# The state rows of an attention kernel with two MoE layers: the last four batch rows multiplied by the weights together in 64-row products, w_in's sums spread unevenly, three sets of PSUM banks

## The chip, the cores and the metric

The kernel runs on one core of a Trainium2 chip. TensorE (PE) multiplies, VectorE (DVE), ScalarE (ACT) and GpSimd (POOL) do the elementwise work, and all DMAs are issued by SyncE (SP). The metric is device time in microseconds (us) for one execution; lower is better. Every product of two float32 operands is made of three products of "fp32r" parts: each operand is split into a rounded high part and the low rest, and high·high, high·low and low·high are added in PSUM. TensorE's time is therefore mostly a count of 512-column matmuls, three for each product.

## What is computed

The reference, cut: cross attention between 512 tokens and 32 state rows per batch row and head, then a gated layer, then a second layer with a softmax gate and a normalisation.

```
x: 8 x 8 x 512 x 64 (batch B, head H, token, D)   state: 8 x 8 x 32 x 64
scores = x @ state.T / 8;    a  = softmax(scores);   xread = a @ state
scores2 = state @ x.T / 8;   a2 = softmax(scores2);  sread = a2 @ x
x = concat([xread, sread], axis=2) -> (8*544, 512)
x = (sigmoid(x @ w_gate) * (x @ w_val)) @ w_out            # 512 -> 1536 -> 512
h = x @ w_in                                               # 512 -> 1024
solu = h * softmax(h);  out = layernorm(solu) * g_ln @ w_out2    # 1024 -> 512
```

## The kernel before

**Stages.** A start-up stage loads and unpacks the weights and treats batch row 0. Then come blocks: rows 1 to 6, a block called SREAD (the 256 `sread` rows of all batch rows), and row 7, which I call the last block. A block runs over 12 chunks `c` of 128 hidden columns. After the last block comes the second layer, over 34 tiles of 128 tokens: four tiles of row 7 first, whose order the scheduler sets, then pairs of tiles in an order written by hand. In the blocks too the order on each engine is that of the program (`tc.manual_schedule`), so one late instruction holds up everything behind it on its engine.

**A chunk.** `first_mm` makes the gate's 128 x 512 product in PSUM bank `gps` and the value's in `vps`, 6 matmuls each. Its stationary operands `mh` and `ml` are not the weights but "states by weights": since xread = a @ state, the kernel multiplies the state rows of a batch row by w_gate and w_val beforehand (`state_w`, one of 12 products `n` = (p, g) of 128 x 512 for each batch row). `sigma` (ACT) reads `gps`, `gated` (DVE) reads `vps`; `gated_hi` (ACT) and `gated_lo` (DVE) split the result into `gh` and `gl`, and one chunk later `out_acc` adds it to the four banks `acc[0..3]` with 12 matmuls (`m` = 0 to 3). A step of the next row's attention (`parts[c]`) stands in each of the first ten chunks; step 4 holds the exponentials, which fill ACT. Its loads (`load_xq` into `e2t`, `load_row`) are issued by SP.

**States by weights.** `make` calls `state_w` at most once a chunk and stays at most three products ahead of their use. Rows 2 to 7 go in pairs: in the even row's turn the state blocks of two batch rows and of two heads fill the 128 x 128 stationary tile `sth`/`stl`, and two `mm3` (6 matmuls of 512 columns) give the product for both rows. Half of the contraction meets zeros there (`a_state_pair_split` fills only the blocks that belong together). What belongs to the odd row goes to DRAM (`msp`) by two 64-partition DMAs, and comes back by one 128-partition DMA (`state_load`) when that row needs it.

**The last block** also unpacks w_out2 (`conv.step`: four DVE instructions, some on ACT, and one POOL addition for each chunk, L223) and prepares sums of blocks of w_in (`w_pair_ops`: 24 steps, each with one DVE instruction, L644, L647 or L652), two for each chunk.

**The second layer.** `h2_out(i, f)` names the two banks of tile `i`. The first four tiles alternate between acc[0..1] and acc[2..3]; `chain(i)` (ACT and DVE) reads them. The pairs after them alternate between `[acc[0], acc[1], acc[2]]` and `[acc[3], gps, vps]`.

Of the kernel before, what the change touches and what calls it, by code (L numbers as in the profile page):

```python
# [19 lines left out]
EXPS = 7  # L20

# [5 lines left out]
def attn_moe_moe2_kernel(ctx: ExitStack, tc: tile.TileContext, x, state, w_gate, w_val, w_out, w_in2, w_out2, g_ln, out):  # L27
# [89 lines left out]
    ssp = tc.dram_tile([B, P, KC * NS], F32, name="ssp")  # L117
    msp = [tc.dram_tile([NF1, P, 512], F32, name=f"msp{b}") for b in range(B)]
# [172 lines left out]
    def paired(a):  # L291
        return 2 <= a < B and a - a % 2 + 1 < B
# [214 lines left out]
    def state_w(b, p, g, i, o, hi, o2=vps):  # L507
# [4 lines left out]
        if not paired(b):  # L512
# [3 lines left out]
        elif b % 2 == 0:  # L516
# [14 lines left out]
    def state_load(b, n):  # L531
        nc.sync.dma_start(out=spill[n % 4], in_=msp[b][n])
# [39 lines left out]
    def out_acc(c, n):  # L572
        h, l = woh[c], wol[c]
        i = c % 2
        for m in range(KC):
            sl = slice(m * P, (m + 1) * P)
            mm3(ps_acc(m, n), h[:, sl], l[:, sl], gh[i][:, 0:n], gl[i][:, 0:n], c == 0, c == NF1 - 1)
# [95 lines left out]
    def banks(i):  # L673
        return ([acc[0], acc[1], acc[2]], [acc[3], gps, vps])[i // 2 % 2]

    def h2_out(i, f):
        if tiles[i][0] == 0:
            return acc[2 * (i % 2) + f]
        a, b, c = banks(i)
        return ((b, c), (a, acc[3] if i + 1 == len(tiles) else b))[i % 2][f]  # L680
# [68 lines left out]
    def turn(i):  # L749
# [3 lines left out]
        if i >= nt - 2:  # L753
            for q, o in ((0, gps), (1, vps)):
# [71 lines left out]

    def loads(n):

        nonlocal loaded
        loaded = max(loaded, made - NF1)  # L830
        while loaded < min(made - NF1 + n, len(ring)):
            b, p, g = ring[loaded]
            if not paired(b) or b % 2 == 0:
                return
            state_load(b, 2 * p + g)
            loaded += 1
# [173 lines left out]
    with tc.manual_schedule():  # L1010
        for n_b, b in enumerate(blocks[1:], 1):
# [5 lines left out]
            if last:  # L1017
# [8 lines left out]
                x_late.close()  # L1026
                sbt = ctx.enter_context(tc.tile_pool(name="sbt", bufs=1, side="right"))
# [8 lines left out]
            nxt = blocks[n_b + 1] if not last else None  # L1036
            for c in range(NF1):
# [41 lines left out]
                if last:  # L1079
                    for _ in range(min(2, len(w_steps) - 1)):  # L1080
# [47 lines left out]
    with tc.manual_schedule():  # L1128
        for i in range(len(first), nt, 2):
# [33 lines left out]
            if end:  # L1163
                product(i, 7, o, False, False)
                plus(acc[3], o, tmp)
# [35 lines left out]
        for f in range(2):  # L1201
            d = slice(f * DO // 2, (f + 1) * DO // 2)
            out2(nt - 1, d=d, bank=(acc[0], att[(nt - 1) % 2])[f])
            store(nt - 1, d, (acc[0], att[(nt - 1) % 2])[f])
# [29 lines left out]
```

## Time and profile before

| what | value |
|---|---|
| median of 3 runs | 1124.13 us (1120.77 to 1129.18) |
| the profiled execution: its time, its span | 1122.8 us, 1121.0 us |
| PE busy | 1081.3 us (96%) |
| DVE, ACT, POOL busy | 773.3 (69%), 601.1 (54%), 384.0 (34%) us |
| mean granted TensorE clock | 0.996 of full speed |
| PE's share of the chain that ended last | 78% |

The profiled execution's time is 1.8 us above its span; the span runs from the first to the last instruction. Matmuls are pipelined: one of 512 columns is listed with some 390 ns, while the next one starts 227 ns later, so steps from start to start count, not durations.

### The profile page before, as it was taken

The numbers are of one execution on the slowest core, as the hardware profiler recorded it, in microseconds if no ns is written. First come the engines' busy times: TensorE is split into PE (matmuls) and PEld (weight loads), VectorE is DVE, ScalarE is ACT, GpSimd is POOL, SyncE is SP. The second block draws the span as 40 slices with busy tenths as digits, with TensorE's granted clock in tenths as the row PEclk, the third lists the DMA queues.
The fourth block names the chain that finished last, engine by engine and source line by source line (L and its number), as shares of the span: only waits on it lengthen the run. The fifth ranks groups of instructions, "written<-read, shape, count | busy, mean of one in ns | idle before, by whom it ended". The sixth has DMA issues, their size and how long they took to land.

```text
span 1121.0 us, 15909 instructions
## 1 busy us (share of the span) xinstructions
PE 1081.3 (96%) x5501; PEld 860.1 (77%) x5501; DVE 773.3 (69%) x1348; ACT 601.1 (54%) x1169; POOL 384.0 (34%) x445
## 2 busy tenths in 40 slices
PE   7787899999999999999999999989999999999998
PEld 5555567777878878878778898867888888888887
DVE  5999956367465476465575466997577777788773
ACT  5766545555445455543554454655565565565553
POOL 2777733300000000000000042226566666767551
PEclk9999999999999999999999999999999999999999
DMA  8764040231360331440521525411454453543441
GB/s 231 244 200 126 1 116 1 71 94 38 78 162 23 81 94 38 121 123 13 133 47 39 158 100 150 113 57 46 143 170 131 158 171 123 176 155 123 158 141 38
DMA packets 139600, 122.88 MB, mean 110 GB/s; under 512 B 71040, under 2 KB 111232, under 8 KB 139520
## 3 DMA queue, kind: packets, MB, share of 16 engines
q1 hardware_dynamic: 139520, 121.87, 37.0%
q8 instruction: 43, 0.70, 0.3%
q14 instruction: 37, 0.30, 0.1%
HBM read 78.32 MB, written 43.52 MB: 109 GB/s over the span
## 4 chain that ended last, share of the span: by engine, by line
PE 78%; DVE 13%; issue 3%; ACT 2%; DMA 1%; POOL 1%; SPq 0%; DVEq 0%; POOLq 0%; ACTq 0%
PE acc L138 11%; PE acc L140 10%; PE acc L139 10%; PE att L138 6%; PE att L140 6%; PE att L139 6%; PE gps L138 4%; PE gps L139 4%; PE gps L140 4%; PE vps L138 4%; PE vps L140 4%; PE vps L139 4%; DVE wf L213 2%; DVE wf L203 1%; DVE wf L206 1%
## 5 line engine op out<-in xcount | busy, mean ns | idle before, releaser
L138 PE MATMUL acc<-gh,woh 128*128 128x512 f32 (+1 forms) x432 | 168.6, 390 | 0.2 <-ACT gh L129 0.2
L139 PE MATMUL acc<-gl,woh 128*128 128x512 f32 (+1 forms) x432 | 164.7, 381 | 2.0 <-POOL gl L570 1.3
L564 DVE TENSOR_TENSOR sg<-vps,sg 128x512 f32<-128x512 f32 (+1 forms) x108 | 71.0, 658 | 135.4 <-PE vps L140 121.5
L140 PE MATMUL acc<-gh,wol 128*128 128x512 f32 (+1 forms) x432 | 164.3, 380 | 0.0
L560 ACT ACTIVATE sg<-gps 128x512 f32<-128x512 f32 (+1 forms) x108 | 61.6, 570 | 151.7 <-PE gps L140 147.2
L138 PEld LDWEIGHTS acc<-gh,woh 128*128 128x128 f32 x432 | 81.7, 189 | 31.4 <-issue 15.4
L223 POOL TENSOR_TENSOR tt<-tt,xn 128x512 int32<-128x512 int32 x16 | 23.5, 1466 | 215.5 <-PE vps L140 153.3
L139 PEld LDWEIGHTS acc<-gl,woh 128*128 128x128 f32 x432 | 81.8, 189 | 18.3 <-POOL gl L570 2.3
L256 POOL MEMSET xtr<- 32x256 f32 x18 | 5.4, 302 | 262.1 <-PE att L324 261.5
L140 PEld LDWEIGHTS acc<-gh,wol 128*128 128x128 f32 x432 | 81.7, 189 | 16.0
L129 ACT ACTIVATE gh<-sg 128x512 fp32r<-128x512 f32 (+1 forms) x101 | 60.4, 598 | 61.8 <-DVE sg L564 61.8
L775 POOL TENSOR_TENSOR wol<-ut,woh 128x512 fp32r<-128x512 f32 x48 | 61.6, 1299 | 86.9 <-ACT woh L129 86.9
L135 DVE TENSOR_TENSOR ml<-gps,mh 64x512 fp32r<-64x512 f32 (+2 forms) x57 | 38.7, 678 | 63.1 <-ACT stg L129 50.9
L138 PE MATMUL gps<-ah,mh 128*128 128x512 f32 x192 | 75.8, 395 | 5.1 <-DVE ml L135 3.9
L129 ACT ACTIVATE mh<-gps 64x512 fp32r<-64x512 f32 (+2 forms) x53 | 31.2, 589 | 90.7 <-PE gps L140 60.5
L138 PE MATMUL att<-woh,woh 128*128 128x512 f32 (+1 forms) x204 | 79.8, 391 | 0.0
L140 PE MATMUL att<-woh,wol 128*128 128x512 f32 (+1 forms) x204 | 79.4, 389 | 0.0
L139 PE MATMUL att<-wol,woh 128*128 128x512 f32 (+1 forms) x204 | 79.3, 389 | 0.0
L140 PE MATMUL gps<-ah,ml 128*128 128x512 f32 x192 | 75.4, 393 | 3.4 <-DVE ml L135 3.2
L138 PE MATMUL vps<-ah,mh 128*128 128x512 f32 x192 | 75.6, 394 | 1.1 <-DVE ml L135 1.1
L139 PE MATMUL gps<-al,mh 128*128 128x512 f32 x192 | 75.2, 392 | 0.9 <-DVE al L135 0.9
L570 DVE TENSOR_TENSOR gl<-sg,gh 128x512 fp32r<-128x512 f32 (+1 forms) x97 | 68.1, 702 | 10.9 <-ACT gh L129 6.9
(431 smaller groups left out, 2875.5 us busy)
## 6 DMA issues: line engine op xcount, KB each, us to landing
usp<-ub SPq DMA_DIRECT2D x32, 512.0 KB, 2.6
ut<-usp SPq DMA_DIRECT2D x128, 128.0 KB, 2.9
msp<-stg SPq DMA_DIRECT2D x72, 128.0 KB, 2.3
stg<-msp SPq DMA_DIRECT2D x36, 256.0 KB, 3.0
out_dram<-sg SPq DMA_DIRECT2D x32, 256.0 KB, 3.0
xn<-in_x_dram SPq DMA_DIRECT2D x15, 512.0 KB, 5.1
e2t<-in_x_dram SPq DMA_DIRECT2D x96, 64.0 KB, 2.7
stge<-in_moe_w_out_dram SPq DMA_DIRECT2D x10, 512.0 KB, 3.6
```

The source lines that it names most:

```text
L129: return act(dst, src, AF.Copy)
L135: return vec.tensor_tensor(out=dst, in0=src, in1=r(hi), op=ALU.subtract)
L138: mm(o, lh, rh, start=start, stop=False, **kw)
L139: mm(o, lh, rl, start=False, stop=False, **kw)
L140: return mm(o, ll, rh, start=False, stop=stop, **kw)
L203: vec.tensor_scalar(out=t, in0=t, scalar1=EXP_LO, scalar2=EXP_HI, op0=ALU.max, op1=ALU.min)
L213: vec.scalar_tensor_tensor(out=tu, in0=hi, scalar=0xC0000000, in1=tu, op0=ALU.bitwise_and, op1=ALU.bitwise_or)
L223: pool.tensor_tensor(out=ti, in0=ti, in1=lo, op=ALU.add)
L560: act(sg[c % 2][:, 0:n], gps[:, 0:n], AF.Sigmoid)
L564: vec.tensor_tensor(out=g, in0=vps[:, 0:n], in1=g, op=ALU.mult)
L570: eng.tensor_tensor(out=gl[c % 2][:, 0:n], in0=sg[c % 2][:, 0:n], in1=r(gh[c % 2][:, 0:n]), op=ALU.subtract)
L775: pool.tensor_tensor(out=lv, in0=wv[:, 4 * q:4 * q + 4], in1=r(hv), op=ALU.subtract)
```

## The change

Three things are changed. First, only rows 2 and 3 go as a pair (`paired`). The states of rows 4 to 7 (`QUAD = 4`) are loaded as one 128 x 512 tile `qst`, transposed and split in the last chunk of row 2's block (`quad_t`, `quad_split`), so that `sth[:, k, :]` holds two heads (64 partitions each) for four batch rows (128 columns). `quad_w` then makes for each of 24 weight tiles (p, k) two products of 64 contraction rows, partitions 0 to 63 and 64 to 127, interleaved matmul by matmul, into two banks. ACT copies one bank to SBUF and DVE the other, and SP stores both to DRAM (`qsp`). 17 of the 24 are in row 3's block and 7 in row 4's, between `out_acc`'s steps, none in chunk 4. `state_load` for rows 4 to 7 then gathers one product by four DMAs of 32 partitions. Second, the 24 steps of w_in's sums go 3, 3, 1, 2, 1, 2, 1, 2, 1, 2, 3, 2 over the chunks (and one behind). Third, the second layer's first tiles use three pairs of banks, and the banks of the rest are renamed to fit.

```diff
+QUAD = 4
+    qsp = [tc.dram_tile([H, P, 512], F32, name=f"qsp{p}") for p in range(NF1 // 2)]
     def paired(a):
-        return 2 <= a < B and a - a % 2 + 1 < B
+        return 2 <= a < QUAD
...
     def state_load(b, n):
-        nc.sync.dma_start(out=spill[n % 4], in_=msp[b][n])
+        if b < QUAD:
+            nc.sync.dma_start(out=spill[n % 4], in_=msp[b][n])
+            return
+        p, g = divmod(n, 2)
+        assert not quads or quads[0] > (p, 2 * g + 1)
+        for h in range(4):
+            r0 = NS * (b - QUAD)
+            nc.sync.dma_start(out=spill[n % 4][NS * h:NS * h + NS], in_=qsp[p][4 * g + h, r0:r0 + NS])
...
+    def quad_t(o):
+        for k in range(KC):
+            nc.tensor.transpose(o[:, k * P:(k + 1) * P], qst[:, k * P:(k + 1) * P], ident)
+
+    def quad_split(o):
+        put(o, *[x.rearrange("p k n -> p (k n)") for x in (sth, stl)])
+
+    def quad_w(pks, os):
+
+        hs = [slice(64 * i, 64 * i + 64) for i in range(2)]
+        for (p, k), o2 in zip(pks, os):
+            w1, w2 = wpart(xe, p, k), wpart(xo, p, k)
+            for n, (s, w) in enumerate(((sth, w1), (sth, w2), (stl, w1))):
+                for o, h in zip(o2, hs):
+                    mm(o, s[h, k, :], w[h], start=n == 0, stop=n == 2)
+        for j, ((p, k), o2) in enumerate(zip(pks, os)):
+            for i, o in enumerate(o2):
+                s = spill4[2 * (k % 2) + i]
+                if i == 0:
+                    act(s, o, AF.Copy)
+                else:
+                    vec.tensor_copy(out=s, in_=o)
+                nc.sync.dma_start(out=qsp[p][2 * k + i], in_=s)
...
     def banks(i):
-        return ([acc[0], acc[1], acc[2]], [acc[3], gps, vps])[i // 2 % 2]
+        return ([acc[2], acc[3], gps], [acc[0], acc[1], vps])[i // 2 % 2]
     def h2_out(i, f):
         if tiles[i][0] == 0:
-            return acc[2 * (i % 2) + f]
+            return (acc[0:2], acc[2:4], [gps, vps])[i % 3][f]
...
-                if c > 0:
-                    out_acc(c - 1, n)
-                else:
-                    out_acc(NF1 - 1, n_before)
+                if n_b == 2 and c == NF1 - 1:
+                    quad_t(att[0])
+                    quad_split(att[0])
+                many = {QUAD - 1: (1, 1, 2, 2, 0, 2, 2, 1, 1, 1, 2, 2), QUAD: (1, 1, 1, 1, 0, 1, 1, 1)}.get(n_b, ())[c:c + 1]
+                many = many[0] if many else 0
+                for m in range(KC):
+                    if m == 2 and many == 2 and c in (5, 6, 10, 11):
+                        quad_w([quads.pop(0), quads.pop(0)], [(gps, vps), att])
+                    elif many == 1 and m == 2 or many == 2 and c < 5 and m % 2:
+                        quad_w([quads.pop(0)], [(gps, vps)])
+                    out_acc(c - 1 if c > 0 else NF1 - 1, n if c > 0 else n_before, [m])
...
                 if last:
-                    for _ in range(min(2, len(w_steps) - 1)):
+                    for _ in range((3, 3, 1, 2, 1, 2, 1, 2, 1, 2, 3, 2)[c]):
                         w_steps.pop(0)()
```

The change moves instructions; three places show how. On PE, in chunk 10 of row 3's block, behind the value's product (`vps<-ah`) stood row 4's pair product, and `out_acc` (`acc<-gh`, `acc<-gl`) followed it. Before:

```order
L140 MATMUL vps<-ah_90,ml 128x512
L138 MATMUL gps<-xe_1199,sth 128x512
L139 MATMUL gps<-xo_1200,sth 128x512
L140 MATMUL gps<-xe_1199,stl 128x512
L138 MATMUL att_181<-xe_1199,sth 128x512
L139 MATMUL att_181<-xo_1200,sth 128x512
L140 MATMUL att_181<-xe_1199,stl 128x512
L138 MATMUL acc_174<-gh_96,woh_74 128x512
L139 MATMUL acc_174<-gl_98,woh_74 128x512
L140 MATMUL acc_174<-gh_96,wol_86 128x512
```

In the same chunk now (xe and xo are the high and low parts of the weights, att two more banks):

```order
L142 MATMUL acc_175<-gh_96,wol_86 128x512
L563 MATMUL gps<-xe_1541,sth 128x512
L563 MATMUL vps<-xe_1541,sth 128x512
L563 MATMUL gps<-xo_1542,sth 128x512
L563 MATMUL vps<-xo_1542,sth 128x512
L563 MATMUL gps<-xe_1541,stl 128x512
L563 MATMUL vps<-xe_1541,stl 128x512
L563 MATMUL att_180<-xe_1541,sth 128x512
L563 MATMUL att_181<-xe_1541,sth 128x512
L563 MATMUL att_180<-xo_1542,sth 128x512
L563 MATMUL att_181<-xo_1542,sth 128x512
L563 MATMUL att_180<-xe_1541,stl 128x512
```

The pair product is gone from its place ahead of `out_acc`, and two four-row products of six 64-row matmuls stand between `out_acc`'s second and third step.

On DVE, in chunk 6 of the last block, from w_out2's split (`wol`) through the unpacking of the next tile (`tt`) and the steps of w_in's sums (`T4l`, `bf`) to the next chunk's `gated` (`sg<-vps`) and the split of its state product (`ml`). Before:

```order
L235 SCALAR_TENSOR_TENSOR wol_80<-tt_104,glnt,woh_68 128x512
L203 TENSOR_SCALAR tt_103<-tt_103 128x512
L206 TENSOR_SCALAR tt_103<-tt_103 128x512
L213 SCALAR_TENSOR_TENSOR tt_103<-xn_99,tt_103 128x512
L652 TENSOR_TENSOR T4l_5312<-bf_5332,T4h_5311 128x512
L644 TENSOR_TENSOR bf_5335<-xe_1199,xo_1200 128x512
L564 TENSOR_TENSOR sg_110<-vps,sg_110 128x512
L135 TENSOR_TENSOR ml<-stg_111,mh 128x512
```

The same chunk now:

```order
L237 SCALAR_TENSOR_TENSOR wol_80<-tt_104,glnt,woh_68 128x512
L205 TENSOR_SCALAR tt_103<-tt_103 128x512
L208 TENSOR_SCALAR tt_103<-tt_103 128x512
L215 SCALAR_TENSOR_TENSOR tt_103<-xn_99,tt_103 128x512
L691 TENSOR_TENSOR T4l_5406<-bf_5426,T4h_5405 128x512
L603 TENSOR_TENSOR sg_110<-vps,sg_110 128x512
L137 TENSOR_TENSOR ml<-stg_111,mh 128x512
```

One step of the sums has left this chunk, so `gated` follows one instruction earlier.

On SP, at the start of row 5's block, between the stores of the block before (`ysp`) and the loads of the next row's tokens (`e2t`). Before:

```order
L586 DMA ysp_188<-tt_103 128x512
L586 DMA ysp_188<-ee_105 128x512
L586 DMA ysp_188<-ee_106 128x512
L586 DMA ysp_188<-tt_104 128x512
L532 DMA stg_111<-msp_199 128x512 x2
L278 DMA e2t_107<-in_x_dram 32x16x32 x4
L278 DMA e2t_108<-in_x_dram 32x16x32 x4
```

The same place now:

```order
L625 DMA ysp_188<-tt_103 128x512
L625 DMA ysp_188<-ee_105 128x512
L625 DMA ysp_188<-ee_106 128x512
L625 DMA ysp_188<-tt_104 128x512
L541 DMA stg_111<-qsp_196 32x512 x8
L280 DMA e2t_107<-in_x_dram 32x16x32 x4
L280 DMA e2t_108<-in_x_dram 32x16x32 x4
```

Eight loads of 32 partitions stand where two of 128 stood, ahead of the token loads.

## Rows read from the trace of the kernel before

**Rows 1.** The page: busy us by engine, share of the span, instructions.

```profile
PE 1081.3 (96%) x5501; PEld 860.1 (77%) x5501; DVE 773.3 (69%) x1348; ACT 601.1 (54%) x1169; POOL 384.0 (34%) x445
```

**Rows 2.** Windows, row 4's block: start:end, length, busy us of each engine.

```profile
385.79:471.50 85.71, 85.56 (x436) 67.78 (x435) 50.51 (x85) 43.77 (x80) 1.21 (x4) 1.00 0.32 80
```

**Rows 3.** Waits of PE, 680 to 790 us: us in total, times, longest.

```profile
PE gps L140 <- DVE ml L135: 3.2, 2, 1.6
PE acc L138 <- DVE xn L719: 1.2, 1, 1.2
```

**Rows 4.** Timeline of PE, one pair product: start, us, engine, line, operation.

```profile
381.51 0.40 PE L138 MATMUL gps<-xe,sth 128*128 128x512 f32 x1
...
382.90 0.40 PE L138 MATMUL acc<-gh,woh 128*128 128x512 f32 x1
```

**Rows 5.** Instructions of line 138 on PE, 374 to 617 us: min/median/max ns.

```profile
L138 PE MATMUL gps<-xe,sth x24: 388/438/506, 374.6 to 615.9; 128*128 128x512 f32 x24
```

**Rows 6.** Timeline of PE around 64-row transposes in row 4's block.

```profile
388.16 0.39 PE L140 MATMUL vps<-ah,ml 128*128 128x512 f32 x1
388.48 0.46 PE L286 MATMUL att<-ident,xtr 64*128 64x64 f32 x4
...
389.21 0.40 PE L139 MATMUL gps<-xo,sth 128*128 128x512 f32 x1
```

**Rows 7.** The same in row 3's block, eight transposes.

```profile
314.11 0.39 PE L140 MATMUL vps<-ah,ml 128*128 128x512 f32 x1
314.43 0.71 PE L286 MATMUL att<-ident,xtr 64*128 64x64 f32 x8
...
315.41 0.40 PE L139 MATMUL acc<-gl,woh 128*128 128x512 f32 x1
```

**Rows 8.** Timeline of PE around the scores: 64-column products, two column halves.

```profile
332.56 0.39 PE L140 MATMUL vps<-ah,ml 128*128 128x512 f32 x1
332.88 1.08 PE L324 MATMUL att<-xtr,stt 128*64 128x512 f32 x4
...
334.22 0.39 PE L139 MATMUL acc<-gl,woh 128*128 128x512 f32 x1
```

**Rows 9.** The same, only what starts before 333.10 us.

```profile
332.88 0.65 PE L324 MATMUL att<-xtr,stt 128*64 128x512 f32 x2
```

**Rows 10.** Timeline of all engines in the last block (PEld: weight loads).

```profile
721.65 0.39 PE L138 MATMUL acc<-gh,woh 128*128 128x512 f32 x1
721.65 0.19 PEld L139 LDWEIGHTS acc<-gl,woh 128*128 128x128 f32 x1
...
722.08 0.68 DVE L647 TENSOR_TENSOR bf<-bf,bf 128x512 f32<-128x512 f32 x1
...
722.30 1.63 POOL L223 TENSOR_TENSOR tt<-tt,xn 128x512 int32<-128x512 int32 x1 [4.88 <-DVE tt L213]
...
722.68 1.79 DVE L644 TENSOR_TENSOR bf<-xe,xo 128x512 f32<-128x512 f32 x1
...
723.69 0.39 PE L138 MATMUL gps<-ah,mh 128*128 128x512 f32 x1
```

**Rows 11.** Timeline of DVE in the last block, `gated` of chunks 5 and 10.

```profile
717.89 0.68 DVE L564 TENSOR_TENSOR sg<-vps,sg 128x512 f32<-128x512 f32 x1
...
750.42 0.68 DVE L564 TENSOR_TENSOR sg<-vps,sg 128x512 f32<-128x512 f32 x1
```

**Rows 12.** Copies of a bank to SBUF on DVE (line 585): min/median/max ns.

```profile
L585 DVE COPY tt<-acc x7: 415/673/675, 151.4 to 691.7; 128x512 f32<-128x512 f32 x6, 128x256 f32<-128x256 f32 x1
```

**Rows 13.** Timeline of SP at the start of row 5's block.

```profile
479.87 1.04 SPq L532 DMA_DIRECT2D stg<-msp  x2
480.95 4.26 SPq L278 DMA_DIRECT2D e2t<-in_x_dram  x8
```

**Rows 14.** Timeline of DVE behind it: the transposes of `e2t`.

```profile
489.30 1.30 DVE L320 STREAM_TRANSPOSE xtr<-e2t 128x512 f32<-128x512 f32 x2
```

**Rows 15.** DMA issues: KB each, median us from issue to landing.

```profile
e2t<-in_x_dram SPq DMA_DIRECT2D x96, 64.0 KB, 2.7
```

More of the change, by code (lines that the diff above doesn't have):

```diff
@@ L511, in state_w @@
         s = spill[n % 4]
-        if not paired(b):
+        if b < 2:
             for q in range(2):
@@ L515, in state_w @@
             put(o, h, l, hi)
-        elif b % 2 == 0:
+        elif b < QUAD and b % 2 == 0:
             for q, o in enumerate((gps, o2)):
@@ L531, in state_load, with quad_load @@
     def state_load(b, n):
-        nc.sync.dma_start(out=spill[n % 4], in_=msp[b][n])
+        if b < QUAD:
[6 more added lines that the diff above has]
+            nc.sync.dma_start(out=spill[n % 4][NS * h:NS * h + NS], in_=qsp[p][4 * g + h, r0:r0 + NS])
+    def quad_load():
+        for a in range(QUAD, B):
+            r0 = NS * (a - QUAD)
+            nc.sync.dma_start(out=qst[r0:r0 + NS].rearrange("n (h d) -> n h d", h=H), in_=state[a].rearrange("h n d -> n h d"))
+    def quad_t(o):
[18 more added lines that the diff above has]
+                nc.sync.dma_start(out=qsp[p][2 * k + i], in_=s)
     def state_w1(c, o=gps, t=slice(0, 2), hi=hi_of):
@@ L570, in gated_lo, with out_acc @@
         eng.tensor_tensor(out=gl[c % 2][:, 0:n], in0=sg[c % 2][:, 0:n], in1=r(gh[c % 2][:, 0:n]), op=ALU.subtract)
-    def out_acc(c, n):
+    def out_acc(c, n, ms=range(KC)):
         h, l = woh[c], wol[c]
         i = c % 2
-        for m in range(KC):
+        for m in ms:
             sl = slice(m * P, (m + 1) * P)
@@ L753, in turn @@
         if i >= nt - 2:
-            for q, o in ((0, gps), (1, vps)):
+            for q, o in ((0, acc[0]), (1, vps)):
                 for j in range(4):
@@ L825, in make @@
             n -= 1
+    quads = [(p, k) for p in range(NF1 // 2) for k in range(KC)]
     def loads(n):
@@ L832, in loads @@
             b, p, g = ring[loaded]
-            if not paired(b) or b % 2 == 0:
+            if b < 2 or paired(b) and b % 2 == 0 or b >= QUAD and quads and quads[0] <= (p, 2 * g + 1):
                 return
@@ L1036, in attn_moe_moe2_kernel @@
             nxt = blocks[n_b + 1] if not last else None
+            if n_b == 2:
+                q_pool = ExitStack()
+                sbq = q_pool.enter_context(tc.tile_pool(name="sbq", bufs=1))
+                qst = sbq.tile([P, 512], F32, name="qst")
+                quad_load()
+            if n_b == 3:
+                spill4 = [qst, *[sbq.tile([P, 512], F32, name=f"qst{i}") for i in range(3)]]
             for c in range(NF1):
@@ L1164, in attn_moe_moe2_kernel @@
                 product(i, 7, o, False, False)
-                plus(acc[3], o, tmp)
+                plus(acc[1], o, tmp)
                 h_max(i + 1, 1)
```

7 lines of the change are left out of this document (4 added, 3 removed).

## The prediction

> **What bounds the kernel now.** I read the page first: TensorE is busy for 96% of the span, every other engine for 69% or less [rows 1]. A busy PE need not be PE at its peak, so the second view is a window on one block, and there the reader sees 85.56 us of matmul in 85.71 [rows 2]. In the attention blocks the time is therefore the count of matmuls times their step of 0.227 us, which is the distance between two starts and not the listed 0.39: one starts at 721.65 and the ninth behind it at 723.69 [rows 10]. The third view is the list of PE's waits. From the last block on it has two entries that matter: 3.2 us in two waits for `ml` from DVE in the last block, and one of 1.2 us for DVE at the first tiles of the second layer [rows 3]. So the change touches three things: a count of matmuls, a stretch where DVE is late, and one bank that is read too long.
>
> **Part A, the products for rows 4 to 7.** *Removed.* One pair product starts at 381.51 and what follows it at 382.90: 1.39 us for six matmuls [rows 4]. Rows 4 to 7 have 24 of them (the list shows 24 first matmuls from 374.6 us on, all of them behind row 2's pair) [rows 5]. They lie on the path, because PE does not stand still there: 24 x 1.39 = 33.4 us.
>
> *Added.* 24 products of six 64-row matmuls. The price depends on whether the two row halves run at the same time. No 64-row pair stands in the trace; the nearest rows are the scores, which use 64-column halves: of the four long matmuls two have already started before 333.10 us and end with the first, 0.65 us in all [rows 8, 9]. Four of them, with all that entering and leaving costs, take 334.22 - 332.56 - 2 x 0.227 = 1.21 us, half of four one after the other at 0.48 to 0.62. I take the same for row halves: 0.227 us for a pair, 3 x 0.227 = 0.68 for a product, 16.3 us for all 24. The other end is one after the other, 0.454 us for a pair; below a full-width matmul's step I see no end, since a half streams the same 512 columns.
>
> *Changing the shape.* PE pays when it goes from full-width to 64-row matmuls and back. The transposes of state rows are such 64-row work: 388.16 to 389.21 is 1.05 us with four of them [rows 6], 314.11 to 315.41 is 1.30 with eight [rows 7]. So one is worth 0.0625, and 1.05 - 0.25 - 2 x 0.227 = 0.35 us is the price of one visit. The new products come in 20 visits: 16 with one product and 4 with two (chunks 5, 6, 10 and 11 of row 3's block). 20 x 0.35 = 6.9 us. Two of the old visits lose four transposes each (rows 5 and 7 no longer load their state block, 8 x 0.0625 = 0.5), and `quad_t` adds four full transposes; I set these against each other.
>
> *Around it.* Each product adds one copy on ACT and one on DVE, 0.67 us on DVE [rows 12], and takes away the pair's four halves of a copy. In row 4's block DVE has 50.5 of 85.7 us of work [rows 2], so the sum of its work is no limit; its order may be. The copies stand ahead of `gated_hi` and `gated_lo`. These are needed one chunk later, behind 12 matmuls of `first_mm` (2.7 us), and copy, split and subtraction take some 2 us: covered. In chunks 2 and 3 two products share `gps` and `vps`, with one `out_acc` step (0.68 us) between the second one and the next `first_mm`; the copy needs 0.67 and a start, so I expect 0.2 to 0.4 us lost there twice, and the first product of chunk 2 may wait as long for `gated`. SP gets more to issue: 48 stores, and 192 loads in place of 48 transfers by rows 4 to 7. An issue takes 0.52 us (two in 1.04) [rows 13]. At the start of rows 5 and 6, eight loads stand where two or none stood, ahead of the token loads, which take 4.26 us to issue and 2.7 to land [rows 13, 15]. They were all issued by 485.2 and landed by 488; DVE needs them at 489.30 [rows 14]. Six more issues are 3.1 us, so DVE will stand for some 1.5 us in these two blocks. Behind that wait are `a_cols` and the `gated` of chunk 3, whose result PE needs four microseconds later; the scores of chunk 3 need the transposes too, and there the slack is about used up. I put all new waits together at 1 us, with 0 and 4 us as ends.
>
> A = -33.4 + 16.3 + 6.9 + 1.0 = -9.2 us.
>
> **Part B, w_in's sums.** From chunk 5 to chunk 10 of the last block `gated` follows itself every (750.42 - 717.89) / 5 = 6.51 us [rows 11], while 24 matmuls need 24 x 0.227 = 5.45. DVE sets the pace. Two steps of the sums stand in each of these chunks. One takes 0.60 us from start to start (722.08 to 722.68); the second reads and writes SBUF while POOL works from 722.30 on, and takes 1.79 instead of 0.68 [rows 10]. A chunk with one step therefore saves at least 0.60 us, and up to 1.4 if the instruction that then meets POOL is `gated`, which reads PSUM. Chunks 2, 4, 6 and 8 lose one step each. Over chunks 2 to 9 DVE fell behind by 8 x 1.06 = 8.5 us at most; that becomes 8.5 - 4 x (0.60 to 1.38) = 3.0 to 6.1. PE lost 3.2 us of idle time plus some 0.3 of pipeline on it [rows 3], so about 5 us were absorbed by the products made ahead, and 0 to 1.1 us stay. The two steps that move into chunks 0 and 1 meet no w_out2 work (its unpacking begins in chunk 2), and those of chunks 10 and 11 come when it has ended. B = -3.0, ends -2.0 and -3.5.
>
> **Part C, the banks.** The third tile of the second layer wrote acc[0] while `chain(0)` still read it: PE idle for 1.2 us until DVE's `xn` [rows 3], and 0.39 - 0.227 = 0.16 lost in the pipeline (a wait is counted from the listed end). The tile now has `gps` and `vps` to itself. C = -1.2, ends -1.4 and 0 (if another of the chain's steps, the turn through DRAM for instance, is next). The other renamed banks keep their distance of two tiles: nothing.
>
> **Sum.** -9.2 - 3.0 - 1.2 = -13.4 us. From the profiled execution's 1122.8 that is 1109.4; the median of the runs is 1.3 us higher, so I forecast 1110.5 us, 1.2% faster. The ends of the parts give 1110.5 - 1.0 - 0.5 - 0.2 = 1108.8 and 1110.5 + 3.0 + 1.0 + 1.2 = 1115.7.
>
> **The rivals.** *The halves run one after the other* (1): 144 x 0.227 = 32.7 in place of 16.3 makes A = +7.2 and the time 1127 us. For it: no row shows two row halves at once. Against it: column halves do [rows 9].
>
> *The weight loads are not hidden* (2). Each 64-row matmul needs its own load of 128 columns. If a load had to wait for the matmul in its own half, a pair would take 0.227 + 0.19 (the load's time in [rows 10]) = 0.42, A = -33.4 + 72 x 0.417 + 6.9 + 1 = +4.5, 1124 us. Against it: the next load starts with the running matmul at 721.65, in the same rows of the array [rows 10], and eight transposes, each with its own load, come every 0.0625 us [rows 6, 7].
> The Trainium skill (TensorE: Matmul & The Clock Gate, Part 3, "What overlaps and what doesn't") states exactly this: a weight load overlaps a running matmul only when the row group differs. The trace disagrees for full-width matmuls; for 64-row ones no row decides.
>
> *Each change of half drains PE* (3), the one that ends slower. The visit price of 0.35 has two ends; if each of the 144 changes between halves cost its entering part, 388.48 - 388.16 - 0.227 = 0.09 us [rows 6], and nothing overlapped, A would be -33.4 + 144 x 0.317 + 20 x 0.26 + 1 = +18.4, and the time 1138 us. It decides from 0.30 us for a single 64-row matmul on: there A eats up B and C and is 1% over. Against it: the two column halves of the scores start together [rows 9].
>
> *SP is late* (4): if loads from `qsp`, four issues each, come too late for `put`, or if the token loads come 3 us later than I think, PE waits in three blocks: 3 x 3 = 9 us, 1119.5 us.
>
> **How the numbers follow.** The runs before spread from 1120.77 to 1129.18, 0.75%, so about 1% (11.2 us, 1112.9) is what this measurement tells from no change. Chances: my forecast 0.76, of which about 0.56 falls below 1112.9 and 0.20 above; rival 4 0.09, rival 2 0.05, rival 1 0.06 (all within 1%), rival 3 0.04 (slower). A little of what is left for "slower" comes from rival 1 with waits on top. Faster by over 1% 0.56, within 1% 0.39, slower 0.05. The range that leaves out at most 2 in 10 reaches from 1104, a little below the ends of my case for the spread of the runs, to 1120, which takes in rival 4.
>
> **What will show it.** In the trace after, the two first 64-row matmuls of a visit should start within a few hundredths of a microsecond of each other, a product should take 0.68 us within a visit, and a visit of one product 1.03 from what it displaces. The blocks of rows 5 and 6 should be 12 x 1.39 = 16.7 us shorter together, and those of rows 3 and 4, which lose as much and get 23.2, some 6.5 us longer. PE's waits for `ml` in the last block should fall from 3.2 to below 1.2 us and the one for `xn` be gone. If the waits of `xtr<-e2t` for its DMA grow and the scores' with them, rival 4 is at work. I am wrong if a pair takes over 0.3 us, or if PE's idle time in the blocks of rows 3 to 6, next to none now, grows beyond 4 us.

## The result, and the profile after

The changed kernel takes 1111.88 us (median of 4 runs, 1110.9 to 1113.68) against 1123.57 for the kernel before (4 runs, 1120.77 to 1129.18): ratio 0.9892, 95% interval 0.9851 to 0.9932. The forecast was 1110.5. The profiled execution is the slowest of the four, 1113.68 us with a span of 1111.8, so the two spans differ by 9.2 us where the medians differ by 11.7.

The page's busy times after, which answer to [rows 1]: PE is busy for 1.9 us less in a span that is 9.2 shorter.

```profile
PE 1079.4 (97%) x5497; PEld 848.5 (76%) x5497; DVE 760.7 (68%) x1335; ACT 577.1 (52%) x1120; POOL 383.5 (34%) x441
```

To see where the time went, I cut both traces at the first `sigma` of each block; the last block ends where its last matmul starts. Windows of the kernel before: rows 3 to 6, SREAD, the last block (start:end, length, busy us of PE, PEld, DVE, ACT, POOL, then granted clock, DMA share, GB/s).

```profile
313.24:387.23 73.99, 73.99 (x391) 59.05 (x390) 42.60 (x77) 33.30 (x64) 0.61 (x2) 1.00 0.34 87
387.23:472.93 85.70, 85.55 (x436) 67.74 (x435) 50.59 (x84) 43.77 (x81) 1.21 (x4) 1.00 0.33 79
472.93:546.91 73.98, 73.98 (x391) 59.06 (x390) 42.60 (x77) 33.28 (x63) 0.60 (x2) 1.00 0.32 85
546.91:632.65 85.74, 85.58 (x443) 68.06 (x442) 50.72 (x86) 43.86 (x83) 0.00 (x0) 1.00 0.27 69
632.65:688.03 55.38, 54.44 (x428) 51.98 (x427) 33.50 (x55) 25.38 (x53) 20.79 (x16) 1.00 0.41 129
688.03:758.83 70.80, 67.09 (x294) 53.48 (x292) 62.76 (x92) 39.90 (x72) 13.05 (x8) 1.00 0.34 101
```

The same six blocks in the changed kernel:

```profile
314.80:404.33 89.53, 88.98 (x478) 64.03 (x477) 50.60 (x87) 37.99 (x71) 0.61 (x2) 1.00 0.53 164
404.33:483.06 78.73, 78.73 (x418) 59.39 (x417) 46.22 (x80) 32.43 (x61) 0.61 (x2) 1.00 0.49 143
483.06:553.97 70.91, 70.91 (x376) 56.54 (x375) 40.39 (x71) 29.16 (x53) 0.61 (x2) 1.00 0.35 91
553.97:624.94 70.97, 70.97 (x383) 56.88 (x382) 40.45 (x73) 29.30 (x55) 0.00 (x0) 1.00 0.29 76
624.94:681.88 56.94, 55.43 (x428) 52.13 (x427) 34.09 (x54) 25.33 (x53) 20.83 (x16) 1.00 0.40 126
681.88:748.69 66.81, 65.81 (x294) 53.77 (x292) 59.13 (x91) 39.62 (x71) 13.10 (x8) 1.00 0.37 106
```

The lengths tell the account:

| stretch | before | after | change |
|---|---|---|---|
| up to row 3's first sigma | 313.24 | 314.80 | +1.56 |
| rows 3 to 6 | 319.41 | 310.14 | -9.27 |
| SREAD | 55.38 | 56.94 | +1.56 |
| last block | 70.80 | 66.81 | -3.99 |
| second layer, to the end | 362.17 | 363.11 | +0.94 |
| span | 1121.0 | 1111.8 | -9.2 |

Of the first line 0.49 us is `quad_t` and `quad_split` in row 2's last chunk; 1.1 is in the start-up stage, where nothing changed: its first `sigma` stands at 30.67 us before and at 31.80 after, and anywhere from 28.6 to 32.3 us in the profiles of the experiments. Counted from there, the two profiles are 10.3 us apart. So part A took 9.3 us from rows 3 to 6, and gave 0.5 and 1.6 back at two other places; part B took 4.0; behind the last block nothing was won.

The second view is the timeline of PE around one product in row 3's block. It answers to [rows 4] and [rows 6].

```profile
325.42 0.40 PE L142 MATMUL acc<-gh,wol 128*128 128x512 f32 x1
325.75 0.50 PE L563 MATMUL gps<-xe,sth 64*128 64x512 f32 x1
325.75 0.50 PE L563 MATMUL vps<-xe,sth 64*128 64x512 f32 x1
326.09 0.39 PE L563 MATMUL gps<-xo,sth 64*128 64x512 f32 x1
326.10 0.39 PE L563 MATMUL vps<-xo,sth 64*128 64x512 f32 x1
326.32 0.39 PE L563 MATMUL gps<-xe,stl 64*128 64x512 f32 x1
326.33 0.39 PE L563 MATMUL vps<-xe,stl 64*128 64x512 f32 x1
326.65 0.50 PE L140 MATMUL acc<-gh,woh 128*128 128x512 f32 x1
326.99 0.40 PE L141 MATMUL acc<-gl,woh 128*128 128x512 f32 x1
```

The two halves start together, pair by pair. From the last full-width matmul ahead to the second one behind there are five steps: 0.33, 0.34, 0.23, 0.33, 0.34, together 1.57. Two of these would be there without the visit (2 x 0.227), so the visit costs 1.11 us: 0.68 for three pairs and 0.43 for coming and going, 0.10 or 0.11 in each of four steps. All 16 visits with one product cost 1.10 to 1.12, but for one of 1.34; the four with two cost 1.79 to 1.80; the sum of the 20 is 25.1 us.

The weight loads in the same visit (PEld):

```profile
326.10 0.18 PEld L563 LDWEIGHTS gps<-xe,stl 64*128 64x128 f32 x1
326.10 0.18 PEld L563 LDWEIGHTS vps<-xe,stl 64*128 64x128 f32 x1
```

The loads of the third pair start with the matmuls of the second pair, in the same halves; they are hidden. Here the Trainium skill (TensorE: Matmul & The Clock Gate, Part 3, "What overlaps and what doesn't") states that a load overlaps a running matmul only in another row group, while the paragraph "The mechanism" ahead of it also names a background weight buffer; this trace disagrees with the first statement for 64-row matmuls, as [rows 10] did for full ones.

PE's waits from 680 to 800 us in the changed kernel, which answer to [rows 3]:

```profile
PE acc L140 <- ACT gh L131: 0.7, 1, 0.7
PE att L142 <- POOL wol L814: 0.6, 1, 0.6
...
```

`ml` (3.2 us) and `xn` (1.2 us) are gone. In their places stand a wait for `gh` at the end of the last block and one in the second layer for an operand of the product that follows the chain, `out2`. The lines left out are 0.2 or 0.3 us each.

Last, SP at the start of the SREAD block. Before:

```profile
637.84 0.94 SPq L532 DMA_DIRECT2D stg<-msp  x2
638.89 10.53 SPq L179 DMA_DIRECT2D xn<-in_moe_w_in_dram  x3
```

In the changed kernel, with one of ACT's waits in this block:

```profile
630.13 4.42 SPq L541 DMA_DIRECT2D stg<-qsp  x8
634.59 13.49 SPq L181 DMA_DIRECT2D xn<-in_moe_w_in_dram  x4
...
ACT tt L197 <- DMA xn<-in_moe_w_in_dram: 1.8, 1, 1.8
```

Eight issues of 0.55 us stand ahead of the first loads of w_in; before, two did (0.94 us in all). ACT then waits 1.8 us for the first tile of w_in, where it waited 0.4.

### The profile page after: what moved, and what is told of

Same layout as the page of the kernel before. It is cut to its first block, busy times and chain, and to the rows that moved or that the text cites. A ratio compares the mean times of both kernels' runs of the same rounds, so it can differ in the third digit from the quotient of the medians.

```text
span 1111.8 us, 16156 instructions
## 1 busy us (share of the span) xinstructions
PE 1079.4 (97%) x5497; PEld 848.5 (76%) x5497; DVE 760.7 (68%) x1335; ACT 577.1 (52%) x1120; POOL 383.5 (34%) x441
## 4 chain that ended last, share of the span: by engine, by line
PE 74%; DVE 15%; issue 3%; DMA 3%; ACT 2%; SPq 2%; POOL 1%; DVEq 0%; POOLq 0%; ACTq 0%
PE acc L140 10%; PE acc L142 9%; PE acc L141 9%; PE att L142 5%; PE att L140 5%; PE att L141 5%; PE gps L140 4%; PE gps L141 4%; PE gps L142 4%; PE vps L140 4%; PE vps L141 4%; PE vps L142 4%; DVE wf L215 2%; DVE wf L205 2%; DVE wf L208 1%
## 5 line engine op out<-in xcount | busy, mean ns | idle before, releaser
L140 PE MATMUL acc<-gh,woh 128*128 128x512 f32 (+1 forms) x432 | 172.5, 399 | 0.7 <-ACT gh L131 0.7
L142 PE MATMUL vps<-ah,ml 128*128 128x512 f32 x192 | 75.2, 392 | 0.0
L141 PE MATMUL vps<-al,mh 128*128 128x512 f32 x192 | 75.0, 391 | 0.0
```

The source lines that it names most:

```text
L140: mm(o, lh, rh, start=start, stop=False, **kw)
L141: mm(o, lh, rl, start=False, stop=False, **kw)
L142: return mm(o, ll, rh, start=False, stop=stop, **kw)
```

## The experiments

Each kernel is compared with the kernel before on the same chip, whose medians were 1122.12 (halves apart, A, B and C undone), 1121.98 (same half, w_in first, one load, visits joined) and 1123.18 us (the other four). The changed kernel itself was run only beside the four runs of the kernel before given above. A difference from it by medians is therefore good to some 1.6 us, by which the medians of the kernel before differ (1121.98 to 1123.57); below that the windows of the traces decide.

**The two halves one after the other in the program.** In `quad_w`:

```diff
-                for n, (s, w) in enumerate(((sth, w1), (sth, w2), (stl, w1))):
-                    for o, h in zip(o2, hs):
+            for o, h in zip(o2, hs):
+                for n, (s, w) in enumerate(((sth, w1), (sth, w2), (stl, w1))):
```

> The changed kernel, but quad_w makes first the three matmuls of one row half and then the three of the other, instead of taking turns. Nothing else moves. Theory (the products are cheap because the two halves stream at the same time): only the matmuls around the change of half can still overlap, so a product needs up to six steps of 0.227 us in place of three; 24 x 3 x 0.227 = 16.3 us more at most, some 1124 to 1128 us. Rival (the products are cheap for another reason, say that a 64-row matmul is shorter, or the gain lies in the removed pair products alone and the rest hides): within 3 us of the changed kernel, 1112 to 1115 us.

Measured: 1110.43 us (1109.63 to 1114.53), ratio 0.9906 (0.9892 to 0.9921): no change. My theory as put there fell. But the rival's reason isn't the right one either, as the timeline of PE in this kernel shows, where the program has gps, gps, gps, vps, vps, vps:

```profile
326.39 0.50 PE L563 MATMUL gps<-xe,sth 64*128 64x512 f32 x1
326.40 0.50 PE L563 MATMUL vps<-xe,sth 64*128 64x512 f32 x1
326.73 0.39 PE L563 MATMUL gps<-xo,sth 64*128 64x512 f32 x1
326.74 0.39 PE L563 MATMUL vps<-xo,sth 64*128 64x512 f32 x1
```

The fourth matmul of the program starts 10 ns after the first and 0.33 us ahead of the second, here and in 19 of the 20 visits. The halves run side by side whichever way they are written. The Trainium skill (TensorE: Matmul & The Clock Gate, Part 3, "What overlaps and what doesn't") states that matmuls start and end in program order; these rows disagree for matmuls in different row halves, and so does the time, since in program order at least two steps of 0.227 us would have been added to each of the 20 visits, 9 us in all.

**Both products in the same half.** In `quad_w`:

```diff
-        hs = [slice(64 * i, 64 * i + 64) for i in range(2)]
+        hs = [slice(0, 64) for i in range(2)]
```

> The changed kernel, but both 64-row products of a weight tile use partitions 0 to 63 of the states and of the weights, so that all six matmuls sit in the same half of the array's rows. Left out of the computation: the products of the odd heads of rows 4 to 7, in whose place those of the even heads stand; the counts and sizes of all instructions are the same. The first experiment left open whether the halves really stream side by side, since it moved nothing by changing their order in the program. Theory (each half is a stream of its own, and the second one is free): now 6 steps of 0.227 us in place of 3, 24 x 3 x 0.227 = 16.3 us slower than the changed kernel, 1128 us. Rival (a 64-row matmul takes half a step whatever its half): no change, 1112 us.

Measured: 1128.06 us (1127.0 to 1129.14), 16.2 above the changed kernel. The visits now take 41.4 us in all instead of 25.1. Timeline of PE:

```profile
325.29 0.50 PE L563 MATMUL gps<-xe,sth 64*128 64x512 f32 x1
325.63 0.39 PE L563 MATMUL vps<-xe,sth 64*128 64x512 f32 x1
325.86 0.39 PE L563 MATMUL gps<-xo,sth 64*128 64x512 f32 x1
326.09 0.39 PE L563 MATMUL vps<-xo,sth 64*128 64x512 f32 x1
```

Two 64-row matmuls in the same half take a full step of 0.23 us each; the second one is free only in the other half. Without that, the change would have been slower than before (ratio 1.005, 1.0033 to 1.0066), as the prediction's first rival had it.

**Six and six.** In the four visits with two products, all six matmuls of one half come first:

```diff
+        for i, h in enumerate(hs):
+            for (p, k), o2 in zip(pks, os):
+                w1, w2 = wpart(xe, p, k), wpart(xo, p, k)
+                for n, (s, w) in enumerate(((sth, w1), (sth, w2), (stl, w1))):
+                    mm(o2[i], s[h, k, :], w[h], start=n == 0, stop=n == 2)
```

> The changed kernel, but in quad_w all matmuls of one row half come first, those of both products where a visit has two, and then all of the other: 16 visits with three and three as in the first experiment, and 4 with six and six. It asks how far ahead PE takes a matmul of the other half. Theory (at least three ahead, as the first experiment's visits showed, and no limit near): the four visits stay at 1.80 us and the first matmul of the second half starts within 0.03 us of the first one; 1111 to 1112 us. Rival (there is a limit between three and six): it starts 0.2 to 0.7 us later, each of the four visits is longer by that, 1 to 3 us in all.

Measured: 1114.09 us (1112.2 to 1115.53), and the four visits take 2.37 us each instead of 1.80, +2.3 in all: the rival. PE, the first five starts of one such visit (the program has six of one half, three on gps and three on att, and then the six of the other, first those on vps):

```profile
353.39 0.50 PE L563 MATMUL gps<-xe,sth 64*128 64x512 f32 x1
353.73 0.40 PE L563 MATMUL gps<-xo,sth 64*128 64x512 f32 x1
353.97 0.39 PE L563 MATMUL gps<-xe,stl 64*128 64x512 f32 x1
353.98 0.50 PE L563 MATMUL vps<-xe,sth 64*128 64x512 f32 x1
354.20 0.39 PE L563 MATMUL att<-xe,sth 64*128 64x512 f32 x1
```

The other half's first matmul, seventh in the program, starts with the third, 0.59 us late. With three in front it started at once; with six it did not. So the order in `quad_w` is free for one product, not for two.

**Part A undone** (`QUAD = 8`, no four-row products; parts B and C stay):

```diff
-QUAD = 4
+QUAD = 8
...
-    quads = [(p, k) for p in range(NF1 // 2) for k in range(KC)]
+    quads = []
...
```

> The changed kernel with the states of rows 4 to 7 in pairs, as before (part A undone; parts B and C stay). The prediction's part A: 9.2 us slower than the changed kernel, 1121.1 us. Theory now, from the stages of the two traces (rows 3 to 6 shorter by 9.3, row 2's block longer by 0.5, the SREAD block longer by 1.5): 7.3 us slower, 1119.2 us, with an SREAD block of 55.4 us again. Rival (the longer SREAD block has nothing to do with part A): 8.8 us slower and an SREAD block of 56.9 us.

Measured: 1119.01 us (1117.47 to 1120.41), ratio 0.9967 (0.9953 to 0.9981). That is 7.1 us above the changed kernel by medians, 8.4 by the two ratios. The windows agree with the lower one: rows 3 to 6 back at 319.41 - 310.14 = 9.3 us more, row 2's block 0.5 less, and SREAD at 55.43, which settles the rival: the longer SREAD block comes with part A. The last block takes 66.82 us here, as in the changed kernel, so its gain does not come from A.

**w_in's first loads ahead of the state loads** in the SREAD block:

```diff
                 if c == 0:
                     y_spill(before, n_before, b)
+                    if b == SREAD:
+                        conv = Conv([...], rings)
+                        conv.load()
+                        conv.load()
                     loads(3)
...
```

> The changed kernel, but in the SREAD block SP issues the first loads of w_in ahead of the state loads, eight issues that now stand before them. Theory (the SREAD block is 1.5 us longer because ACT waits for the first w_in tile, which is issued 3.5 us later): SREAD block 55.4 to 55.6 us, the changed kernel minus 1.4, 1110.5 us. Rival (the block is longer because the state loads are late themselves, or for something on DVE): no change, or a new wait for the split of the state products in the last block, up to 1 us slower.

Measured: 1109.31 us (1108.11 to 1113.42), ratio 0.989 (0.9868 to 0.9912). The window of the SREAD block, and SP in it:

```profile
621.81:677.16 55.35, 54.32 (x428) 51.92 (x427) 33.53 (x54) 25.34 (x53) 20.78 (x16) 1.00 0.42 129
...
627.04 0.91 SPq L181 DMA_DIRECT2D xn<-in_moe_w_in_dram  x2
628.00 6.38 SPq L541 DMA_DIRECT2D stg<-qsp  x8
```

The block is 1.6 us shorter, ACT's wait for `w_in` is gone, and none came in its place. The cause of the 1.6 us is shown: SP's queue.

**One load instead of four.** The four rows' states are interleaved in the stationary tile, so one DMA of 128 partitions gathers a product:

```diff
-        for h in range(4):
-            r0 = NS * (b - QUAD)
-            nc.sync.dma_start(out=spill[n % 4][NS * h:NS * h + NS], in_=qsp[p][4 * g + h, r0:r0 + NS])
+        nc.sync.dma_start(out=spill[n % 4], in_=qsp[p].rearrange("h (n a) f -> a (h n) f", a=B - QUAD)[b - QUAD, P * g:P * g + P])
...
-            nc.sync.dma_start(out=qst[r0:r0 + NS].rearrange("n (h d) -> n h d", h=H), in_=state[a].rearrange("h n d -> n h d"))
+            nc.sync.dma_start(out=qst[a - QUAD:P:B - QUAD].rearrange("n (h d) -> n h d", h=H), in_=state[a].rearrange("h n d -> n h d"))
```

> The changed kernel, but the four rows' states are interleaved in the stationary tile (column 4 n + a in place of 32 a + n), so that the rows of one batch row stand in DRAM at an even distance and a state product comes back by one DMA of 128 partitions in place of four of 32: 48 issues in place of 192, some 0.5 us of SP time each. Theory (the new waits of the changed kernel are SP's lateness: 1.5 us in the SREAD block, 0.7 us for a store's slot in row 3's block, a little on DVE's transposes): 1.5 to 2.3 us less than the changed kernel, 1109.6 to 1110.4 us, SREAD block 55.4 us. Rival (the strided rows cost more on the way or the waits have another cause): no change or slower.

Measured: 1108.93 us (1108.68 to 1109.91), ratio 0.9881 (0.9866 to 0.9896), 3.0 below the changed kernel. Its SREAD block takes 55.09 us, 1.85 less. Row 3's block is 0.87 shorter as well, the wait for a store's slot, but that part doesn't belong to the loads, as a later run shows.

**Visits joined.** In rows 3 and 4 the attention's step moves behind `out_acc`'s first step and a product follows it at once:

```diff
+                late_pe = n_b in (QUAD - 1, QUAD) and c in (0, 1, 3, 8) and not (n_b == QUAD and c == 8)
-                if pe:
+                if pe and not late_pe:
                     pe()
...
                 for m in range(KC):
+                    if late_pe and m == 1:
+                        pe()
+                        quad_w([quads.pop(0)], [(gps, vps)])
...
```

> The changed kernel, but in rows 3 and 4 the step of the next row's attention (four or eight state transposes, scores, sread products; chunks 0, 1, 3, and 8 in row 3 alone) goes behind out_acc's first step, and a four-row product follows it at once, so that PE goes from one kind of partial matmul to the other without full-width matmuls between: 7 visits fewer. Theory (a visit's 0.43 us is paid for leaving the full-width shape and coming back): 7 x 0.43 = 3.0 us less than the changed kernel, 1108.9 us. Rival (every change of shape is paid, from one partial shape to another too): 0 to 1 us less. Second rival (the step of the attention, 0.7 to 1.8 us later, makes the exponentials and with them the split of gh late): slower by up to 2 x 1 us, 1114 us, with PE waiting for gh in chunk 4 or 5.

Measured: 1109.93 us (1108.59 to 1112.19), ratio 0.989 (0.9872 to 0.9908), 2.0 below the changed kernel. Chunk by chunk the seven joined visits save 0.35, 0.22, 0.18 and 0.22 (row 3, chunks 0, 1, 3, 8) and 0.37, 0.23, 0.22 (row 4, chunks 0, 1, 3): 1.8 us, and no new wait. That lies between theory and rival: about half of a visit's 0.43 is saved, more where the product follows transposes. Timeline of PE in row 3, chunk 0:

```profile
314.50 0.46 PE L288 MATMUL att<-ident,xtr 64*128 64x64 f32 x4
314.75 0.49 PE L563 MATMUL vps<-xe,sth 64*128 64x512 f32 x1
314.77 0.48 PE L563 MATMUL gps<-xe,sth 64*128 64x512 f32 x1
```

The Trainium skill (TensorEngine Tiling (Array Packing), "Key Properties") states that changing the tiling mode, not just the tile, drains TensorE. These rows agree: transposes and products are listed with the same shape, 64 rows by 128 columns (64*128), and the products start 0.25 us after the first of four transposes, where four transposes alone take that long. The scores and the `sread` products, which split the columns (128*64 and 128*32), have another shape; from them about half of the price stays.

**Part B undone**, two steps in every chunk:

```diff
-                    for _ in range((3, 3, 1, 2, 1, 2, 1, 2, 1, 2, 3, 2)[c]):
+                    for _ in range(min(2, len(w_steps) - 1)):
```

> The changed kernel with w_in's sums in two steps for every chunk, as before (part B undone). The prediction's part B: 3.0 us slower than the changed kernel (2.0 to 3.5), 1114.9 us. Theory now, from the last block's length in the two traces (70.79 and 66.81 us): 4.0 us slower, 1115.9 us, all of it in chunks 5 to 10 of the last block, and PE's waits for ml back at about 3 us. Rival (the last block is shorter because of something that part A brought, say other state products made ahead): under 1 us slower, 1112 to 1113 us.

Measured: 1115.43 us (1115.2 to 1118.07), ratio 0.9947 (0.9934 to 0.9959), 3.6 above the changed kernel. Its last block and PE's wait in it:

```profile
678.84:749.69 70.85, 67.12 (x294) 53.41 (x292) 62.80 (x92) 39.95 (x72) 13.06 (x8) 1.00 0.33 100
...
PE gps L142 <- DVE ml L137: 3.4, 3, 1.6
```

The 4.0 us and the waits for `ml` are back: part B alone made the last block shorter.

**Part C undone**, the second layer's banks as before:

```diff
-        return ([acc[2], acc[3], gps], [acc[0], acc[1], vps])[i // 2 % 2]
+        return ([acc[0], acc[1], acc[2]], [acc[3], gps, vps])[i // 2 % 2]
...
-            return (acc[0:2], acc[2:4], [gps, vps])[i % 3][f]
+            return acc[2 * (i % 2) + f]
...
```

(and the banks of the rest renamed with them).

> The changed kernel with the second layer's banks as they were before (part C undone), all else as changed. The prediction's part C: 1.2 us slower than the changed kernel, 1113.1 us. Theory now, from the trace of the changed kernel (the wait for xn is gone, but 1.0 us stands a few microseconds later at the first operand of the second product): the same within 0.5 us, with the wait for xn back in the trace and the later one smaller. Rival (the new banks cost something elsewhere in the second layer, which is 0.9 us longer in the changed kernel): up to 1 us faster, 1111 us.

Measured: 1112.34 us (1111.06 to 1115.7), ratio 0.992 (0.9906 to 0.9934). Beside 1111.88 and the 1110.43 of the kernel with the halves apart this tells nothing under 2 us. In the trace the wait for `xn` is back (1.0 us), and the old banks have a new one beside part B, 0.4 us for `ml` at the first product of the second layer.

**The two best together** (one load, visits joined):

> The two experiments that took most off put together: one DMA for each state product (48 issues in place of 192), and seven four-row products joined to a step of the attention. Theory (the two gains add, but for the 0.7 us wait for a store's slot in row 3's block, which both of them took away): 1108.93 - (1.34 + 0.80 - 0.70) = 1107.5 us. Rival (what one of them gives back is the same idle time): 1108.9 us.

Measured: 1106.3 us (1106.06 to 1108.33), ratio 0.985 (0.9827 to 0.9873): faster than both kernels, by 17 and by some 5.6 us. The two gains add: the seven visits save the same as before, chunk by chunk within 0.05 us, and the SREAD block takes 55.05 us. One line of PE's waits, from 390 to 410 us:

```profile
PE gps L140 <- ACT qst L565: 0.7, 1, 0.7
```

This is the wait for a store's slot in row 3's block, back although there is now one load for each product. It was 0.6 us in the changed kernel, and none in the next kernel, which runs the same instructions up to there. So it comes and goes with the transfers, and I had no reason to count it as a gain of the single load.

**The same with the old banks:**

> The kernel of the run before in this list, with the second layer's banks as they were before the change. The prediction's part C: 1.2 us slower than that one. Theory now (in the traces the new banks take 1.3 us away at the third tile and then stand 0.8 us for the operand of the second product and some 1.5 us more up to 150 us later, where the old banks stand 0.4): 0.3 to 0.8 us faster, within what the runs can tell. What decides is the lost time by place in the two traces, with everything ahead of the second layer alike.

Measured: 1107.76 us (1107.42 to 1108.26), ratio 0.9856 (0.9834 to 0.9879), 1.5 above the run before it: against my theory, for the prediction's C, though the two ranges overlap. PE's waits from the last block on:

```profile
PE acc L140 <- DVE xn L755: 1.0, 1, 1.0
...
PE acc L140 <- DVE ml L137: 0.4, 1, 0.4
```

I added up, over all starts of matmuls, what PE lost beyond 0.227 us a step. In the second layer's first 50 us this is 2.8 and 2.5 us in the two kernels with the old banks, and 1.9 to 2.5 in those with the new ones (2.1 in the changed kernel). Behind 50 us it is 0.2 and 1.9 with the old ones, 0.7 to 2.2 with the new ones: what comes late differs from profile to profile of the same instructions, by more than C is worth.

**One step of w_in's sums from chunk 10 to chunk 2:**

```diff
-                    for _ in range((3, 3, 1, 2, 1, 2, 1, 2, 1, 2, 3, 2)[c]):
+                    for _ in range((3, 3, 2, 2, 1, 2, 1, 2, 1, 2, 2, 2)[c]):
```

> The kernel of the first run in this list, with one step of w_in's sums moved from chunk 10 of the last block (three steps) to chunk 2 (one). Theory (in chunk 10 the third step, 0.68 us on DVE, stands ahead of gated, and PE loses 1.5 us at the last out_acc for it): 0.5 us less than that kernel, PE's wait for gh at the end of the last block 0.1 to 0.3 us instead of 0.8. Rival (DVE sets the pace from chunk 2 on, so that a step there comes back as a wait for ml or gl): no change, or 0.6 us slower.

Measured: 1108.1 us (1107.4 to 1108.6), ratio 0.9859 (0.9836 to 0.9881): no gain. The wait for `gh` falls to 0.2, and 0.4 us for `ml` comes in its place at the first product of chunk 10; the last block is 66.59 instead of 66.82 us. The rival holds in its mild form: by this trace DVE has no room for one more step on its way from chunk 2 to chunk 9.

## Why the prediction was right, by its steps

**The mechanism of A was right.** It chose halves at the same time, from the scores' column halves [rows 9]. The trace has them 3 ns apart, and the experiment with one half for both gives 16.2 us for what the prediction priced at 16.3. Rival 1's 1127 us is near the 1128.06 that that kernel measured. Rival 2 is refuted by the hidden weight loads, rival 3 by pairs at 0.23 us.

**A's sum was 2 us too good, by terms of both signs.** Removed: 9.27 + 25.1 (visits) + 0.7 (a wait, below) = 35.1 us and not 33.4. Rows 5 and 6, where nothing was added, are 17.84 us shorter and not 16.7; rows 3 and 4 are 8.57 us longer and not 6.5. Some of the 1.7 us is the transposes that fell away (0.25 us each in rows 3 and 5); 0.6 us is one pair product of row 6 behind the exponentials, where PE stood for `vps` (chunk 5 is 2.00 us shorter instead of 1.39), and as much again is one of row 4 (chunk 5 is 0.87 us shorter there, though a visit of 1.11 us was added). The prediction's 24 equal products did not show these two. Two rows of the kernel before (timeline of PE):

```profile
579.04 0.39 PE L140 MATMUL gps<-xe,stl 128*128 128x512 f32 x1
579.58 0.50 PE L138 MATMUL vps<-xe,sth 128*128 128x512 f32 x1 [0.15 <-DVE sg L564]
```

Added: 25.1 us and not 16.3 + 6.9 = 23.2. The term that was too small is the price of a visit, 0.43 in place of 0.35. The prediction read it from a visit of transposes [rows 6], which it rightly closed at the second full-width matmul behind. One more row of it:

```profile
388.87 0.51 PE L138 MATMUL gps<-xe,sth 128*128 128x512 f32 x1
```

The step in and the step behind the visit are as long there as here (0.32 and 0.34 against 0.33 and 0.34). The difference lies inside. From the first transpose to the first full-width matmul (388.48 to 388.87) it is 0.14 us more than four transposes of 0.0625; from the first pair to the first full-width matmul (325.75 to 326.65) it is 0.22 more than three pairs of 0.227. The second pair is late by 0.11, the second transpose by 0.05. A price read from small matmuls was too low for long ones: 20 x 0.08 = 1.6 us. Waits in rows 3 to 6: the forecast 0.2 to 0.4 us twice in chunks 2 and 3 was 0.24 once, and there was 0.7 for the store's slot (listed as a wait of 0.6). That is 1 us in all, as forecast, but it is not SP's eight loads at the start of rows 5 and 6: these two blocks ran without any wait of PE. Outside these rows: +0.5 for `quad_t`, which was set against the transposes, and +1.6 in SREAD, which had no term at all.

**Rival 4 was right in kind and wrong in place.** SP's eight issues made nothing late for `put` and cost DVE some 2.3 us of harmless waiting for `e2t` in rows 5 and 6. They cost PE 1.6 us where the prediction did not look: in the SREAD block, whose first loads of w_in stand behind them. The prediction walked along SP's queue for the blocks that it spoke of and not for the one after them. A in all: -9.3 + 0.5 + 1.6 = -7.2, against a forecast of -9.2.

**B was larger:** 4.0 us in the trace, 3.6 in the runs, against 3.0 with an end of 3.5. The prediction had PE lose 3.2 us idle and some 0.3 in the pipeline. In the windows above PE's idle time in the last block falls by 2.7 us (3.71 to 1.00), and its listed busy time for the same 294 matmuls by 1.3 (67.09 to 65.81): the 0.3 was the term that was too small. From chunk 5 to chunk 11 of the last block `sigma` follows itself every 5.62 us on average, where it was 6.32 before; the matmuls need 5.45. Of the "0 to 1.1 us" that were to stay nothing stayed on `ml`; what is left is 0.7 for `gh`, behind the third step of chunk 10.

**C was the weak term.** The wait for `xn` went as forecast. But the tile that no longer waits runs into `out2`, whose operand POOL has not made (0.6 us), the "another of the chain's steps" that the prediction kept as its end at 0. The second layer of the profiled execution is 0.9 us longer, its first 50 us cost some 0.5 us less with the new banks than with the old ones beside part B (and no less than in the kernel before, which had no wait for `ml` there). The one pair on the same chip that differs in nothing else says 1.5. Counted from the first `sigma` of the start-up stage, its profiles take 1075.4 and 1076.7 us, the changed kernel and the one with the old banks 1080.0 and 1079.9: 1.3 us for the new banks in one pair, nothing in the other. C lies between 0 and -1.5 and isn't settled more narrowly.

**The time came out near because the errors partly cancel:** A was forecast 2.0 us too good, B 1.0 too small, C up to 1.2 too good. By the traces A and B make -7.2 - 4.0 = -11.2, the medians are 11.7 apart, and the forecast was -13.4 with all three. That it landed 1.4 us from the measured median is in part luck. (By its own figures, 1109.4 + 1.3, the forecast should have read 1110.7 and not 1110.5.)

## What to carry to other kernels

When contraction blocks half filled with zeros can be cut into 64-row products, the second half is free, and what remains is a fixed price for each change of shape: count changes and not matmuls, put partial shapes next to each other, and read the price of a change, up to the second full-width matmul behind it, from a visit whose matmuls are as long as the new ones. When a transfer is split into four, follow the issuing queue past the block that uses it to whatever stands behind it; here the bill of 1.6 us came a block later, and one interleaved layout took it away. When a wait goes, look for the operand that the freed engine reaches next before booking the gain.

## What the runs showed of the hardware

- TensorE starts matmuls in two row halves independently of the order in the program as long as few stand between: with three of the other half in front the fourth started 10 ns after the first, with six in front the seventh 0.59 us after it.
- A 64-row matmul of 512 columns behind one in the same half has the same step as a full one, 0.23 us; only one in the other half comes free (3 ns apart).
- A change from full-width to 64-row matmuls and back costs 0.43 us, spread over four steps of 0.32 to 0.34 instead of 0.227; next to transposes of the same 64 x 128 shape 0.35 of it falls away, next to scores or `sread` products, which split the columns, 0.2.
- SP needed about as long to issue a load of states of 32 partitions (0.55 us, eight in 4.42) as one of 128 (0.47 us, two in 0.94).
